# Transposes of the attention sums in halves, and five edits around the last rounds, in a two-layer attention and Fourier kernel

## The chip, the cores and the metric

The kernel runs on one core of a Trainium2 chip. Times are device microseconds of one execution. The kernel before took 1332.05 us (median of 3 runs, 1330.12 to 1336.22). The profile shown below is of one further execution, which took 1332.09 us by itself; the span in its trace, from the first to the last instruction, is 1330.0 us, so 2.1 us lie outside it.

Six names come back all the time. TensorE (PE in the profile) multiplies; PEld is its loading of weights, which overlaps. VectorE (DVE), ScalarE (ACT) and GpSimd (POOL) do the element work. SyncE (SP) only issues DMAs. PSUM is the memory that TensorE writes to: eight banks of 2 KB per partition, so one bank holds 512 fp32 columns of 128 partitions.

## What is computed

Four residual blocks on a sequence of 2048 tokens of width 576, fp32 throughout: attention A, Fourier filter B, A again, B again, each on the layer-normed input.

```python
def _A_ref(x, wqkv, wo):
    H = 32; Dh = D // H; W = 256
    q, k, v = split_heads(x @ wqkv)
    scores = jnp.einsum("bhqd,bhkd->bhqk", q, k) * (Dh ** -0.5)
    mask = (idx[:, None] - idx[None, :] >= 0) & (idx[:, None] - idx[None, :] < W)
    p = _softmax(jnp.where(mask, scores, -1e9), axis=-1)
    return merge_heads(jnp.einsum("bhqk,bhkd->bhqd", p, v)) @ wo

x = x + _A_ref(_layernorm(x), A_wqkv, A_wo)
x = x + _B_ref(_layernorm(x), B_w_r, B_w_i)   # irfft2(rfft2(x) * (w_r + 1j w_i))
x = x + _A_ref(_layernorm(x), A_wqkv, A_wo)
x = x + _B_ref(_layernorm(x), B_w_r, B_w_i)
```

The 32 heads have 18 channels each, and a query sees itself and the 255 tokens before it.

## The kernel before

The program is written out in one fixed order. Each engine takes its own instructions strictly in that order, and an instruction whose inputs or whose buffer are not ready holds up everything behind it on its engine. SyncE's DMA issues are such a queue too.

One attention layer (`layer_a`) has four stages. First the normed input is transposed and split in a high and a low part, and the values are projected (`vps`, L1005). Then q and k are projected in 9 groups of 128 columns (`proj`, accumulators `pj`, L1109). Their weights are loaded by `w_load` and split by `w_split`, in the order of the groups. Then comes the attention itself, and then the output projection (class `Out`, accumulators `ops`, L802), whose first matmuls (`early`) stand directly behind the last matmul of the attention in TensorE's order.

The attention runs over x = 0 to 127: eight groups n of four heads, times sixteen blocks i of 128 tokens. A block needs, for each of its four heads:

- `score_max` (L1160): TensorE writes the block's scores to a bank with tag S, of which there are three, and VectorE takes the row maximum (L1174). It runs ten blocks ahead of the rest.
- `m_rows` (L1182): after four blocks the maxima are transposed (`tpm`), negated by ScalarE and stored by a DMA on SyncE into a row of q, so that the next multiplication already subtracts them.
- `exps` (L1193): TensorE writes scores with the keys on the partitions to a bank with tag E (three of these, too), ScalarE takes the exponent into P, and GpSimd clears what the mask leaves out (L1208, L1211). In the last ten blocks, when most score maxima are done, the second pair of heads uses S banks instead, but not in the last four blocks of all.
- `part` (L1216): TensorE multiplies P with the values, and the sums of exponents come out as a 19th row. The sums of four blocks of queries stand in the four quarters of **one** bank, U (L1434), which is allocated once: blocks 0 and 1 of four in columns 0 to 255, blocks 2 and 3 in columns 256 to 511.

After the fourth block of a chunk c VectorE transposes the whole of U to `us` in squares of 32 by 32 (L1230), so that tokens come to the partitions. `divide` (L1238) takes the reciprocal of the 19th entry on VectorE and multiplies (GpSimd; VectorE for the last n). `back` (L1244) transposes `us` to `o` on VectorE, `store` (L1248) sends `o` to DRAM on SyncE, and after the fourth chunk of a head group `pack` (L1256) copies its 72 used rows within DRAM, with DMAs on GpSimd's queue. The last head group has no pack; its chunks go straight to the tile `o7`.

Two loops order this work. `bursts` (L1330) goes in rounds of three scores and three exponents; up to x of about 104 each round also has a few of the projection's matmuls, and rounds without any follow. `later` (L1311) sets in which following round divide, back, store and pack of a chunk stand: 1, 3, 4 and about 10 rounds on. From x = 118 (`MIX`) a second loop (L1444) goes block by block: exponents of t, then `pv(t-2)`, which is both parts of block t-2, and the waiting steps in between. No score maxima are left there.

`behind` (L1402) puts the preparation of the output projection beside the last 20 blocks: the weights of the output are loaded and split (`out.split`, five times, at t = 110, 112, ... 118; a copy by ScalarE and a subtraction by GpSimd, L752), the constants of the following transform are loaded into buffers that the q and k weights used before (`out.const`, tags wraw, wqh, wql), the packed rows are fetched (`out.attended`, tile `oraw`, last at t = 121 and 122), and at t = 125, 126 and 127 the first three tiles of them are turned and split by VectorE alone (`out.turn`, L787 to L789). The last instructions of the attention are then `pv(126)`, `pv(127)`, the transpose of the last chunk, and its divide and back.

Of the kernel before, what the change touches and what calls it, by code (L numbers as in the profile page):

```python
# [8 lines left out]
F32 = mybir.dt.float32  # L9
F32R = mybir.dt.float32r  # L10
# [5 lines left out]
S, D = 2048, 576  # L16
DF = 289
NF = 290
NT = 16
# [622 lines left out]
NQ = 8  # L642
# [54 lines left out]
def split_w(nc, raw, h, l, eng_l):  # L697
    nc.scalar.copy(h, raw)
    eng_l.tensor_sub(l, raw, h.bitcast(F32))
# [16 lines left out]
class Out:  # L716
# [32 lines left out]
    def split(self, k):  # L749
        c = slice(2 * self.n * k, 2 * self.n * (k + 1))  # L750
        self.nc.scalar.copy(self.w["h"][:, c], self.raw[:, c])
        self.nc.gpsimd.tensor_sub(self.w["l"][:, c], self.raw[:, c], self.w["h"][:, c].bitcast(F32))  # L752

    def const(self, k):

        t = ("wraw", "wraw", "wqh", "wqh", "wql")[k]
        d = self.bp.tile([128, 2, NF], F32R, tag=t, name=f"dc{k}", bufs=2)
        self.nc.sync.dma_start(d.bitcast(F32), self.dc_d[:, 2 * k:2 * k + 2].bitcast(F32))
        self.dcs.append(d)

# [105 lines left out]
def layer_a(tc, ident, eps, bp, big, src, dst, wqk_d, wv_d, wo_d, dc_d, gc_d, dram, copy, wvs, second, spectral, share):  # L866

    nc = tc.nc
    V, A, T, P = nc.vector, nc.scalar, nc.tensor, nc.gpsimd
# [14 lines left out]
    if True:  # L884
# [7 lines left out]
        wt, wraws = {}, {}  # L892

        def w_load(i):
            raw = bp.tile([128, 5, 128], F32, tag="wraw", name=f"wqr{i}", bufs=2)
            nc.sync.dma_start(raw.rearrange("p a b -> p (a b)"), wqk_d[i])
            wraws[i] = raw

        def w_split(i):
            raw = wraws[i]  # L900
            h = bp.tile([128, 5, 128], F32R, tag="wqh", name=f"wqh{i}", bufs=2)
            l = bp.tile([128, 5, 128], F32R, tag="wql", name=f"wql{i}", bufs=2)
            wt[i] = (h, l)
            split_w(nc, raw, h, l, V if i == 2 else P)
            if i + 2 < 9:
                w_load(i + 2)


        with tc.tile_pool(name="a1", bufs=2) as wp, ExitStack() as banks:
            pps = []  # L910
            if not second:
                wraw = wp.tile([128, 5, D], F32, name="wvraw", bufs=1)
# [163 lines left out]
        with ExitStack() as c2:  # L1076
            wp = c2.enter_context(tc.tile_pool(name="a2", bufs=2))
            pp = Banks(tc, c2, "a2p", ("S", "pj"))
# [16 lines left out]
            def proj(i, c, bank=0):  # L1095
# [5 lines left out]
                def mm(s, k):  # L1101
                    wk, p, xk = k
                    if s == 7 and c == 2 and 0 < i < 8:
                        w_split(i + 1)
# [31 lines left out]
            def stack_load(n, c, some=range(4)):  # L1136

                q, k = qs[n % 2], ks_[n % 2]
                cs = slice(c * 512, c * 512 + 512)
                for which, t, parts in ((0, q, (0, 0, 1)), (1, k, (0, 1, 0))):  # L1140
                    for hp in range(2):
                        if 2 * which + hp not in some:
                            continue
                        r0 = 144 * n + 72 * which + 36 * hp
                        for slot, part in enumerate(parts):
                            b = 64 * hp + 18 * slot
                            (P if which and (n == 0 and c > 1 or n == 1 and c == 0) else nc.sync).dma_start(
                                t[b:b + 18, :, cs].bitcast(F32), qk_d[part, r0:r0 + 36, cs].rearrange("(f d) t -> d f t", f=2).bitcast(F32))
# [44 lines left out]
            def exps(x, pair, hp):  # L1193

                n, j = divmod(x, NT)
                q, k = qs[n % 2], ks_[n % 2]
                nq = min(3, NT - j) * 128
                hl_ = 2 * hp + pair
                if hp == pair == 0:
                    pt[n, j] = wp.tile([128, 4, 384], F32, tag="P", name=f"P{n}_{j}", bufs=6)  # L1200
                p = pt[n, j]

                ps = pp.tile([128, 512], F32, name=f"E{x}_{hl_}", **(dict(tag="S", bufs=3) if pair and NX - LEAD <= x < NX - 4 else dict(tag="E", bufs=3)))
                b = 64 * hp
                T.matmul(ps[:, 0:nq], k[b:b + 64, pair, j * 128:j * 128 + 128], q[b:b + 64, pair, j * 128:j * 128 + nq], start=True, stop=True)  # L1205
                A.activation(p[:, hl_, 0:nq], ps[:, 0:nq], AF.Exp, scale=SC)  # L1206
                if hp == pair == 1:
                    P.affine_select(out=p[:, :, 0:128], in_=p[:, :, 0:128], pattern=[[0, 4], [1, 128]], compare_op=ALU.is_ge,  # L1208
                                    fill=0.0, base=0, channel_multiplier=-1)
                    if nq == 384:  # L1210
                        P.affine_select(out=p[:, :, 256:384], in_=p[:, :, 256:384], pattern=[[0, 4], [-1, 128]], compare_op=ALU.is_gt,  # L1211
                                        fill=0.0, base=0, channel_multiplier=1)

            us = {}

            def part(x, half):  # L1216
                n, i = divmod(x, NT)

                e = i - i % 2
                j = (i - 1, i - 2 + 2 * (i % 2))[half]  # L1220
                q0 = e if j < i else i
                q1 = e + 2 if i - 1 == j else q0 + 1
                for h in range(4):
                    if j >= 0:
                        T.matmul(U[32 * h:32 * h + 19, (q0 % 4) * 128:(q0 % 4) * 128 + 128 * (q1 - q0)], vts[n][:, j, h],  # L1225
                                 pt[n, j][:, h, (q0 - j) * 128:(q1 - j) * 128],
                                 start=j == max(e - 1, 0), stop=j == i or (i == e and j == i - 2), skip_group_check=True)
                if half and i % 4 == 3:
                    us[n, i // 4] = u = wp.tile([128, NT, 32], F32, tag="us", name=f"us{n}_{i}", bufs=1)
                    V.transpose(u, U.rearrange("r (p n) -> r n p", n=NT))  # L1230

            def pv(x):
                part(x, 0)
                part(x, 1)

            os = {}

            def divide(n, c):  # L1238
                u = us[n, c]
                rc = wp.tile([128, NT, 1], F32, tag="rc", name=f"rc{n}_{c}", bufs=2)  # L1240
                V.reciprocal(rc, u[:, :, 18:19])
                (V if n == NQ - 1 else P).tensor_mul(u[:, :, 0:18], u[:, :, 0:18], rc.to_broadcast([128, NT, 18]))

            def back(n, c):  # L1244
                os[n, c] = o = wp.tile([128, NT, 32], F32, tag="o", name=f"o{n}_{c}", bufs=2)
                V.transpose(o, us[n, c])

            def store(n, c, engines=None):  # L1248
                o = os[n, c].rearrange("r n p -> r (n p)")
                if n < NQ - 1:  # L1250
                    nc.sync.dma_start(op_d[n, :, c], o)
                    return
                for h in range(4):
                    (engines[h] if engines else nc.sync).dma_start(out.o7[18 * h:18 * h + 18, 512 * c:512 * c + 512], o[32 * h:32 * h + 18])

            def pack(n, h):  # L1256
                a, b = [f.rearrange("e c x -> (e c x)").rearrange("(a b) -> a b", a=16) for f in (o_d[72 * n + 18 * h:72 * n + 18 * h + 18], op_d[n, 32 * h:32 * h + 18])]
                P.dma_start(a, b)

            for k, (i, c) in enumerate(((0, 0), (1, 0), (0, 1), (1, 1), (0, 2), (0, 3), (1, 2), (1, 3))):  # L1260
                for f in proj(i, c, k % 2):
# [8 lines left out]
            NX = NQ * NT  # L1270
            LEAD = 10
# [37 lines left out]
            steps = {}  # L1309

            def later(k, n, c):  # L1311
                for lag, f in zip(later.lags, (divide, back, store)):
                    steps.setdefault(k + lag, []).append((f, n, c))
                if c == 3:
                    for h in range(4):
                        steps.setdefault(k + (10 + 2 * h if n < NQ - 2 else 9 + h // 2), []).append((pack, n, h))

            later.lags = 1, 3, 4

            def lasting(p):  # L1320
                x, half = p
# [8 lines left out]
            def bursts():  # L1330
# [8 lines left out]
                for k in range(-(-len(es) // 3)):  # L1339
# [6 lines left out]
                    for f in e:  # L1346
                        exps(*f)
# [46 lines left out]
                for p in parts:  # L1394
                    part(*p)
                    if p[1] and p[0] % 4 == 3:
                        later(k, *divmod(p[0] // 4, 4))
# [36 lines left out]
            U = pp.tile([128, 512], F32, tag="U", name="U", bufs=1)  # L1434
# [2 lines left out]
                f()  # L1437
                done += 1
            now = -(-4 * MIX // 3)
            later.lags = 1, 3, 4  # L1440
            ahead = [(max(now, 2 * k - now), f) for k in sorted(steps) for f in steps.pop(k)]
            for k, f in ahead:
                steps.setdefault(k, []).append(f)
# [20 lines left out]

            out.early(0, [bank(k, f"ops0_{k}") for k in ("pj", "S")], slice(0, 4))
            divide(NQ - 1, 3)
            back(NQ - 1, 3)
            store(NQ - 1, 3, (nc.sync, nc.scalar, P, nc.sync))
            out.early(0, None, slice(4, 11))
            out.early(1, [bank("S", f"ops1_{k}") for k in range(2)])  # L1470
# [55 lines left out]
```

## Time and profile before

| | us |
|---|---|
| median of 3 runs | 1332.05 |
| the profiled execution | 1332.09 |
| its span | 1330.0 |
| TensorE busy | 1295.2 |
| VectorE busy | 947.2 |
| first and last transpose of U, first layer (start) | 144.1 and 458.3 |
| last transpose of U, second layer (start) | 1139.6 |
| all waits of U's matmuls for VectorE's transposes (8) | 3.3 |
| all waits of exponent scores for ScalarE (8) | 3.7 |

The granted clock of TensorE is 0.996 on average, so the clock explains nothing here. Two kinds of row are read in the following: rows of the timeline, which give a start, a length, engine, line, operation and tiles, and in square brackets the idle time of the engine before it with what ended that; and rows of windows, which give each engine's busy time in a stretch. The timeline merges neighbours of one kind (x2, x3), and the ends of matmuls in it are modelled. A matmul that waits for a bank while the one before is still counted shows as a longer row and not as idle time.

### The profile page before, as it was taken

How to read it: one execution, taken by the hardware profiler on the slowest of the kernel's cores; microseconds unless marked ns; L12 is line 12 of the kernel's file. 1: busy time of each engine (PE TensorE's matmuls, PEld its weight loads, DVE VectorE, ACT ScalarE, POOL GpSimd, SP SyncE). 2: the span in 40 equal slices, each digit the busy share in tenths (PEclk: the TensorE clock that was granted, in tenths of full speed). 3: DMA queues.
4: the chain of work that ended last, by engine and by line, in shares of the span. 5: the costliest groups of instructions: out<-in, count | busy, mean ns of one | idle time of the engine just before them, and what ended most of it. 6: DMA issues, size and time to landing. Idle time of an engine off the chain costs nothing.

```text
span 1330.0 us, 33103 instructions
## 1 busy us (share of the span) xinstructions
PE 1295.2 (97%) x10911; PEld 957.5 (72%) x10911; DVE 947.2 (71%) x3132; ACT 753.5 (57%) x1896; POOL 721.8 (54%) x1212
## 2 busy tenths in 40 slices
PE   9999999999999899999999999999999999999998
PEld 8986666566665599975999975666656654897587
DVE  5417888888889677766674148988888887675755
ACT  5622776677767645533355415677766678573233
POOL 2258666676667643566221295567667668213721
PEclk9999999999999999999999999999999999999999
DMA  6856766665657747688873468566656659497884
GB/s 205 215 161 204 220 206 190 214 201 186 188 162 241 222 120 227 191 282 254 265 251 76 102 208 225 184 213 178 192 175 192 189 173 296 140 346 254 283 260 155
DMA packets 179487, 274.22 MB, mean 206 GB/s; under 512 B 67743, under 2 KB 77727, under 8 KB 177989
## 3 DMA queue, kind: packets, MB, share of 16 engines
q1 hardware_dynamic: 166751, 242.45, 58.4%
q0 software_dynamic: 4912, 14.62, 4.3%
q10 hardware_dynamic: 7654, 15.03, 3.2%
q8 instruction: 88, 1.44, 0.5%
q14 instruction: 82, 0.67, 0.2%
HBM read 164.54 MB, written 114.81 MB: 210 GB/s over the span
## 4 chain that ended last, share of the span: by engine, by line
PE 82%; DMA 4%; POOL 4%; DVE 3%; issue 3%; ACT 2%; SPq 1%; DVEq 0%; ACTq 0%; POOLq 0%
PE pj L1109 18%; PE S L1172 13%; PE U L1225 11%; PE vps L1005 9%; PE ops L802 7%; PE E L1205 5%; PE po L274 4%; PE pq L524 3%; PE p L503 2%; PE pi L600 2%; PE pf L274 2%; PE pz L312 1%; POOL ks L1266 1%; POOL qs L1267 1%; DMA yd<-ye 1%
## 5 line engine op out<-in xcount | busy, mean ns | idle before, releaser
L1174 DVE CUSTOM_DVE_ANT_0 jk<-S,mask 128x384 bf16<-128x384 f32 (+2 forms) x1024 | 488.2, 525 | 72.3 <-PE S L1172 35.9
L1206 ACT ACTIVATE P<-E 128x384 f32<-128x384 f32 (+2 forms) x1024 | 408.2, 476 | 171.9 <-PE E L1205 134.4
L1172 PE MATMUL S<-ks,qs 63*128 63x384 f32 (+2 forms) x1024 | 280.1, 374 | 1.3 <-POOL qs L1267 0.3
L1208 POOL TENSOR_SCALAR_AFFINE_SELECT P<-P 128x512 f32<-128x512 f32 x256 | 163.2, 638 | 190.6 <-ACT P L1206 173.8
L1205 PE MATMUL E<-qs,ks 64*128 64x384 f32 (+2 forms) x1024 | 224.7, 372 | 6.4 <-ACT P L1206 3.7
L1172 PEld LDWEIGHTS S<-ks,qs 63*128 63x128 f32 x1024 | 145.6, 184 | 115.2 <-DVE m L1174 87.2
L1225 PE MATMUL U<-P,vq 128*19 128x128 f32 (+1 forms) x3840 | 188.6, 328 | 5.1 <-DVE us L1230 3.3
L1109 PE MATMUL pj<-xh,wqh 128*128 128x512 f32 x360 | 155.4, 432 | 0.4 <-DVE sg L1127 0.2
L1225 PEld LDWEIGHTS U<-P,vq 128*19 128x19 f32 x3840 | 95.6, 98 | 82.6 <-issue 16.0
L1211 POOL TENSOR_SCALAR_AFFINE_SELECT P<-P 128x512 f32<-128x512 f32 x224 | 142.8, 637 | 0.0
L1205 PEld LDWEIGHTS E<-qs,ks 64*128 64x128 f32 x1024 | 115.6, 185 | 22.5 <-ACT P L1206 16.5
L1109 PE MATMUL pj<-xh,wql 128*128 128x512 f32 x360 | 122.1, 416 | 0.0
L1109 PE MATMUL pj<-xl,wqh 128*128 128x512 f32 x288 | 119.6, 415 | 0.0
L802 PE MATMUL ops<-oroom 128*128 128x290 f32 (+1 forms) x812 | 114.0, 297 | 1.7 <-DVE ofree L848 1.2
L802 PEld LDWEIGHTS ops<-oroom 128*128 128x128 f32 x812 | 110.4, 189 | 2.3 <-ACT ofree L836 1.4
L1109 PEld LDWEIGHTS pj<-xh,wqh 128*128 128x128 f32 x360 | 67.7, 188 | 31.2 <-issue 14.0
L1174 DVE DVE_READ_ACCUMULATOR2_ANT m<- 128x1 f32 x1024 | 85.1, 83 | 0.0
L1121 ACT CAST sg<-pj 128x512 fp32r<-128x512 f32 x72 | 42.4, 589 | 72.9 <-PE pj L1109 66.8
L1109 PEld LDWEIGHTS pj<-xh,wql 128*128 128x128 f32 x360 | 64.2, 188 | 21.9 <-issue 10.8
L1230 DVE STREAM_TRANSPOSE us<-U 128x512 f32<-128x512 f32 x64 | 45.8, 716 | 35.8 <-PE U L1225 35.8
L1109 PEld LDWEIGHTS pj<-xl,wqh 128*128 128x128 f32 x288 | 54.2, 188 | 16.8 <-issue 9.1
L789 POOL TENSOR_TENSOR oroom<-oraw,oroom 64x128 fp32r<-64x128 f32 x26 | 13.9, 536 | 95.8 <-issue 46.1
(509 smaller groups left out, 2290.9 us busy)
## 6 DMA issues: line engine op xcount, KB each, us to landing
qk_d<-sg SPq DMA_DIRECT2D x56, 512.0 KB
qs<-qk_d SPq DMA_DIRECT2D x384, 72.0 KB
ks<-qk_d SPq DMA_DIRECT2D x348, 72.0 KB
op_d<-o SPq DMA_DIRECT2D x56, 256.0 KB
v_d<-vt SPq DMA_DIRECT2D x32, 304.0 KB
vq<-v_d SPq DMA_DIRECT2D x16, 608.0 KB
wt<-in_w SPq DMA_DIRECT2D x16, 580.0 KB
ofree<-x SPq DMA_DIRECT2D x16, 580.0 KB
```

The costliest lines, as they stand in the source:

```text
L274: T.matmul(ps[:, c, 0:NF], tail[r] if si == 4 else hl_(si), dcs[b // 2][r, b % 2], start=mi == si == 0, stop=si == 4)
L802: self.nc.tensor.matmul(self.ps[u][n][:, 0:self.n], x, self.w[p][:, (2 * wk + n) * self.n:(2 * wk + n + 1) * self.n], start=first and i == ...
L1005: T.matmul(ps[:, n, 0:288], xT(xk, c), w[:, wk, n * 288:(n + 1) * 288], start=i == 0, stop=i == len(ks) - 1)
L1109: T.matmul(box["ps"].rearrange("r (n p) -> r n p", n=NT) if second else box["ps"], w[:, wk], x, start=s == 0, stop=s == len(ks) - 1)
L1172: T.matmul(ps[:, 0:N], q[b:b + 63, pair, i * 128:i * 128 + 128], k[b:b + 63, pair, lo:hi], start=True, stop=True)
L1174: V.tensor_tensor_reduce(out=jk[:, 0:N], in0=ps[:, 0:N], in1=mask[:, 384 - N:384], scale=1.0, scalar=-3e38, op0=ALU.add, op1=ALU.max, accu ...
L1205: T.matmul(ps[:, 0:nq], k[b:b + 64, pair, j * 128:j * 128 + 128], q[b:b + 64, pair, j * 128:j * 128 + nq], start=True, stop=True)
L1206: A.activation(p[:, hl_, 0:nq], ps[:, 0:nq], AF.Exp, scale=SC)
L1208: P.affine_select(out=p[:, :, 0:128], in_=p[:, :, 0:128], pattern=[[0, 4], [1, 128]], compare_op=ALU.is_ge, fill=0.0, base=0, channel_mult ...
L1211: P.affine_select(out=p[:, :, 256:384], in_=p[:, :, 256:384], pattern=[[0, 4], [-1, 128]], compare_op=ALU.is_gt, fill=0.0, base=0, channel ...
L1225: T.matmul(U[32 * h:32 * h + 19, (q0 % 4) * 128:(q0 % 4) * 128 + 128 * (q1 - q0)], vts[n][:, j, h], pt[n, j][:, h, (q0 - j) * 128:(q1 - j) ...
L1230: V.transpose(u, U.rearrange("r (p n) -> r n p", n=NT))
```

## The change

Six things are changed; all of them are in both layers.

1. `part` transposes U after every second block, 256 columns at a time, into one half of `us` (which gets two buffers). `back` does the same: its second half stands one round after the first. Order of columns within the halves is such that `o` is the same as before. U stays one bank.
2. `out.split` subtracts with VectorE for k = 3 and 4 (t = 116 and 118) and with GpSimd for k = 0 to 2 as before.
3. `pack` of the last but one head group (n = 6) is issued by SyncE; all others stay with GpSimd.
4. The second pair's exponents use S banks through the last block.
5. q and k weights: the first two raw tiles get buffers of their own, all others share one buffer, so that a load is issued one split later. This makes room for the second `us`.
6. The transform's constants are spread differently over the freed buffers.

```diff
     def split(self, k):
         c = slice(2 * self.n * k, 2 * self.n * (k + 1))
         self.nc.scalar.copy(self.w["h"][:, c], self.raw[:, c])
-        self.nc.gpsimd.tensor_sub(self.w["l"][:, c], self.raw[:, c], self.w["h"][:, c].bitcast(F32))
+        (self.nc.vector if k > 2 else self.nc.gpsimd).tensor_sub(self.w["l"][:, c], self.raw[:, c], self.w["h"][:, c].bitcast(F32))
...
-        t = ("wraw", "wraw", "wqh", "wqh", "wql")[k]
-        d = self.bp.tile([128, 2, NF], F32R, tag=t, name=f"dc{k}", bufs=2)
+        t = ("wraw", "wqh", "wqh", "wql", "wql")[k]
+        d = self.bp.tile([128, 2, NF], F32R, tag=t, name=f"dc{k}", bufs=2 if k else 1)
...
         def w_load(i):
-            raw = bp.tile([128, 5, 128], F32, tag="wraw", name=f"wqr{i}", bufs=2)
+            raw = wp.tile([128, 5, 128], F32, name=f"wqr{i}", bufs=1) if i < 2 else bp.tile([128, 5, 128], F32, tag="wraw", name=f"wqr{i}", bufs=1)
...
-            if i + 2 < 9:
-                w_load(i + 2)
+            if 0 < i < 8:
+                w_load(i + 1)
...
-                ps = pp.tile([128, 512], F32, name=f"E{x}_{hl_}", **(dict(tag="S", bufs=3) if pair and NX - LEAD <= x < NX - 4 else dict(tag="E", bufs=3)))
+                ps = pp.tile([128, 512], F32, name=f"E{x}_{hl_}", **(dict(tag="S", bufs=3) if pair and NX - LEAD <= x else dict(tag="E", bufs=3)))
...
-                if half and i % 4 == 3:
-                    us[n, i // 4] = u = wp.tile([128, NT, 32], F32, tag="us", name=f"us{n}_{i}", bufs=1)
-                    V.transpose(u, U.rearrange("r (p n) -> r n p", n=NT))
+                if half and i % 2:
+                    c, g = divmod(i // 2, 2)
+                    if g == 0:
+                        us[n, c] = wp.tile([128, NT, 32], F32, tag="us", name=f"us{n}_{c}", bufs=2)
+                    V.transpose(us[n, c][:, 8 * g:8 * g + 8], U[:, 256 * g:256 * g + 256].rearrange("r (p a b) -> r a b p", a=8, b=2))
...
-            def back(n, c):
-                os[n, c] = o = wp.tile([128, NT, 32], F32, tag="o", name=f"o{n}_{c}", bufs=2)
-                V.transpose(o, us[n, c])
+            def back(n, c, g):
+                if g == 0:
+                    os[n, c] = wp.tile([128, NT, 32], F32, tag="o", name=f"o{n}_{c}", bufs=2)
+                V.transpose(os[n, c][:, :, 16 * g:16 * g + 16].rearrange("r (a b) p -> r a b p", b=2), us[n, c][:, 8 * g:8 * g + 8])
...
-                P.dma_start(a, b)
+                (nc.sync if n == NQ - 2 else P).dma_start(a, b)
...
-                for lag, f in zip(later.lags, (divide, back, store)):
-                    steps.setdefault(k + lag, []).append((f, n, c))
+                for lag, f, *g in ((1, divide), (3, back, 0), (4, back, 1), (4, store)):
+                    steps.setdefault(k + lag, []).append((f, n, c, *g))
...
             divide(NQ - 1, 3)
-            back(NQ - 1, 3)
+            for g in range(2):
+                back(NQ - 1, 3, g)
             store(NQ - 1, 3, (nc.sync, nc.scalar, P, nc.sync))
```

2 lines of the change are left out of this document (removed).

## The prediction

> **What bounds the kernel now.** I read the page's busy times first, then windows of 10 to 100 us in the attention, then the timeline of TensorE and VectorE there, then both ends of the attention.
>
> ```profile
> PE 1295.2 (97%) x10911; PEld 957.5 (72%) x10911; DVE 947.2 (71%) x3132; ACT 753.5 (57%) x1896; POOL 721.8 (54%) x1212
> ```
>
> TensorE has only 34.8 us of idle time in the span. All that this change can give must come from there, or from stalls that are counted as busy. Windows (stretch, its length, then busy us with instructions for PE, PEld, DVE, ACT, POOL; clock, DMA share, GB/s) show two regimes:
>
> ```profile
> 300.00:400.00 100.00, 99.77 (x992) 61.05 (x988) 85.97 (x331) 70.41 (x178) 65.30 (x98) 1.00 0.57 177
> ```
> ```profile
> 405.00:415.00 10.00, 9.71 (x122) 5.69 (x123) 9.96 (x40) 7.52 (x19) 8.07 (x14) 1.00 0.64 204
> ```
>
> In the long middle of the attention, where rounds carry projection matmuls, TensorE is full and VectorE has slack. From 405 us, when these matmuls are used up, VectorE is full (9.96 of 10) and TensorE runs at its pace.
>
> Hidden stalls stand in the middle. TensorE's rows of two score matmuls, undisturbed and behind a transpose, and VectorE at that place:
>
> ```profile
> 1006.33 0.34 PE L1172 MATMUL S<-ks,qs 63*128 63x384 f32 x2
> ...
> 1069.39 0.67 PE L1172 MATMUL S<-ks,qs 63*128 63x384 f32 x2
> ```
> ```profile
> 1067.44 0.72 DVE L1230 STREAM_TRANSPOSE us<-U 128x512 f32<-128x512 f32 x1 [0.35 <-PE U L1225]
> 1068.08 0.52 DVE L1174 CUSTOM_DVE_ANT_0 jk<-S,mask 128x384 bf16<-128x384 f32 x1
> ```
>
> The transpose holds VectorE for 0.64 us, the three S banks come free that much later, and the pair of scores takes 0.33 us longer. In the two middles (140 to 395 and 820 to 1085 us) I counted the rows of this kind that are longer than 0.44 us and follow a transpose of `us` or `o` within 3 us, 47 of them, from the first to the last:
>
> ```profile
> 151.72 0.48 PE L1172 MATMUL S<-ks,qs 63*128 63x384 f32 x2
> ...
> 1073.16 0.61 PE L1172 MATMUL S<-ks,qs 63*128 63x384 f32 x2
> ```
>
> What they exceed 0.39 us by sums to 10.5 us.
>
> **The change, part by part.** *Price of a half.* It is not in the trace. The whole and its nearest rows by size:
>
> ```profile
> L1230 DVE STREAM_TRANSPOSE us<-U 128x512 f32<-128x512 f32 x64 | 45.8, 716 | 35.8 <-PE U L1225 35.8
> ```
> ```profile
> L1174 DVE CUSTOM_DVE_ANT_0 jk<-S,mask 128x384 bf16<-128x384 f32 x896 | 448.6, 550 | 50.6 <-PE E L1205 31.9 <-PE S L1172 14.9
> ...
> L1174 DVE CUSTOM_DVE_ANT_0 jk<-S,mask 128x128 bf16<-128x128 f32 x64 | 16.6, 285 | 6.2 <-PE S L1172 6.0
> ```
>
> 256 columns cost 550 - 285 = 265 ns in the maxima. A half then holds VectorE for 0.64 - 0.265 = 0.375 us, and a pair of halves 0.11 us longer than a whole. The bounds are 0.32 (exactly half) and 0.64 (no less than a whole); I take 0.375.
>
> *The middle.* Behind each transpose VectorE is late by 0.27 us less. Cutting each of the 47 excesses by at most 0.27 gives 9.2 us. The new half two rounds earlier falls into time in which VectorE would wait for the next score, as the 0.35 us of idle time ahead of 1067.44 shows. Some excesses are exponents that wait for ScalarE, so I take **-7.5 us**, with -3 and -9.2 as bounds.
>
> *The end of the scores* (405 to 437 us, and the same in the second layer). VectorE has no slack, so work is paid in full: about seven transposes in halves, 7 x 0.11 = 0.8 us, and the subtraction of k = 3, for which a similar row (576 columns, fp32r result) gives 0.75:
>
> ```profile
> L949 DVE TENSOR_TENSOR wv<-wvraw,wv 128x576 fp32r<-128x576 f32 x4 | 2.9, 748 | 0.2 <-ACT wv L946 0.2
> ```
>
> Together +1.5 us per layer. The subtraction of k = 4 comes after the last maximum, where VectorE mostly waits; it costs nothing.
>
> *The last blocks.* TensorE's rows in the first layer:
>
> ```profile
> 446.47 0.41 PE L1225 MATMUL U<-P,vq 128*19 128x128 f32 x8 [0.81 <-POOL P L1208]
> 446.81 0.62 PE L1205 MATMUL E<-qs,ks 64*128 64x384 f32 x4
> ...
> 448.14 1.67 PE L1205 MATMUL E<-qs,ks 64*128 64x384 f32 x4
> ```
>
> GpSimd without two packs and two subtractions ends its mask earlier: up to -0.8. Four exponent scores take 1.67 us where banks are short and 0.62 where not, so S banks give up to -1.05 here. Against the +1.5 that leaves -0.35 by the time block 123 is done.
>
> *A new wait at the very end.* U is one bank. Whether TensorE may write one half while VectorE reads the other is seen in how this program treats other banks. ScalarE, VectorE, then ScalarE and VectorE again:
>
> ```profile
> 487.01 0.74 ACT L291 ACTIVATE yh<-pf,ofree 128x578 fp32r<-128x578 f32 x1 [2.11 <-PE pf L274]
> 487.65 0.64 ACT L293 COPY xf<-pf 128x580 f32<-128x580 f32 x1
> ```
> ```profile
> 488.32 0.82 DVE L294 SCALAR_TENSOR_TENSOR yl<-pf,ofree,yh 128x578 fp32r<-128x578 f32 x1 [0.73 <-ACT xf L293]
> ```
> ```profile
> 1280.73 0.40 ACT L617 COPY bs<-po 128x290 f32<-128x290 f32 x1 [1.27 <-issue]
> 1281.03 0.18 ACT L618 ACTIVATE xo<-po 128x2 f32<-128x2 f32 x1
> ```
> ```profile
> 1281.24 0.46 DVE L619 TENSOR_TENSOR xo<-po,bs 128x287 f32<-128x287 f32 x1 [1.33 <-ACT xo L618]
> ```
>
> L294 needs `yh`, ready at 487.75, yet starts at 488.32, when L293 has ended, which merely reads the same bank. L619 starts behind L618, which reads two other columns of its bank. So accesses of two engines are ordered by bank, not by address, and I take the same for a write by TensorE beside a read by VectorE. The Trainium skill, "PSUM — Partial Sum Buffer", section "PSUM bank collisions raise a hardware error", says so outright: disjoint columns of one bank collide, hardware does not arbitrate, so software must order them. The L619 rows agree for two readers; no run here shows a write. By that rule the sum ends at 1330, without it at the first rival's time.
>
> Earlier halves are covered by the exponent scores that stand between two blocks' parts, and VectorE is free there. But the half of blocks 124 and 125 must end before `pv(126)`. On VectorE it stands behind turns 0 and 1 and ahead of turn 2; behind `pv(126)` and `pv(127)` on TensorE stands the whole output projection. VectorE and TensorE, first layer:
>
> ```profile
> 452.20 0.72 DVE L787 CAST oroom<-oraw 128x512 fp32r<-128x512 f32 x1
> ...
> 454.64 0.71 DVE L1246 STREAM_TRANSPOSE o<-us 128x512 f32<-128x512 f32 x1
> ...
> 456.91 0.43 DVE L787 CAST oroom<-oraw 128x512 fp32r<-128x512 f32 x1
> ...
> 458.28 0.72 DVE L1230 STREAM_TRANSPOSE us<-U 128x512 f32<-128x512 f32 x1
> ```
> ```profile
> 456.55 0.40 PE L802 MATMUL ops_pj<-oroom 128*128 128x288 f32 x1
> ```
> ```profile
> L1225 PE MATMUL U<-P,vq 128*19 128x128 f32 (+1 forms) x3840 | 188.6, 328 | 5.1 <-DVE us L1230 3.3
> ```
>
> Turns 0 and 1 end at 456.9. With -0.35 from above and a transpose of blocks 122 and 123 that is a half (-0.27), plus 0.1 for two backs, this becomes 456.4. The half takes 0.4; the 32 matmuls of two blocks take 32 x 188.6 / 3840 = 1.6. TensorE then begins the projection at 458.4 instead of 456.55: **+1.9 us**, with +0.9 if the turns start 1 us earlier, +3.5 if they come later. In the second layer they start when their data land:
>
> ```profile
> 1134.80 0.56 DVE L787 CAST oroom<-oraw 128x512 fp32r<-128x512 f32 x1 [2.03 <-DMA oraw<-o_d]
> ...
> 1138.26 0.43 DVE L787 CAST oroom<-oraw 128x512 fp32r<-128x512 f32 x1
> ```
> ```profile
> 1137.16 0.40 PE L802 MATMUL ops_pj<-oroom 128*128 128x290 f32 x1
> ```
>
> 1138.26 + 0.4 + 1.6 = 1140.3 instead of 1137.16: +3.1. Whatever ScalarE, GpSimd and S banks save there is lost in this wait. I add 0.4 for landings that follow the later end of the scores: **+3.5 us**, with +1.5 and +6 as bounds.
>
> *Pack by SyncE.* Its four issues pass ahead of the store of chunk (7, 0), one load and `attended(3, ...)` on SyncE, and the first waits for the store of `o`, which now stands a round later. Before, SyncE waited about there already:
>
> ```profile
> SPq L1254 <- DMA op_d<-o: 1.4, 1, 1.4
> ```
>
> I take nothing either way beyond the 0.4 above; the second rival prices it.
>
> *The rest.* One raw weight buffer less means that a load starts one group later, still a whole group (56 matmuls) ahead of its split; the old code's load waited for the same split on SyncE. The constants go to buffers whose readers ended with the projection. Both nothing; a late load would hold ScalarE's copy, once per group. The later back and store delay SyncE's next issue by at most a round.
>
> Sum: -7.5 + 1.9 + 3.5 = -2.1 us. The profiled execution took 1332.09 us, 0.04 from the median, so **1330 us**.
>
> **The rivals.**
>
> *First: halves of U are ordered by address.* For it: the two halves share no byte, and no row shows TensorE and VectorE at odds over a bank's other columns. Against: L294 and L619. Then the end gives instead of taking: -1 in the first layer, and -0.3 (only the last chain's shorter half) in the second, where data land at the same time: -8.8 with some of the middle left, 1324 us.
>
> *Second: packing by SyncE brings the turns' data late*, and it ends slower. The store that the pack needs comes a round (about 2 us: three maxima at 0.5 and part of a transpose) later, SyncE stands still until it has landed, and behind it stand the loads that turn 0 needs. Because of the new wait each us passes to TensorE one to one. It decides once the pack leaves SyncE later than GpSimd issued it; 2 us in the first layer and 2 + 1.4 in the second make +5.4, so 1335.5 us. Against: GpSimd itself issued only between its masks, and SyncE had idle time there.
>
> *Third: the stalls do not go.* If a half holds VectorE as long as a whole (0.64), the middle gives nothing and the ends of the scores pay 7 x 0.265 = 1.9 us more each, of which I count half as the other two waits hide some: 1332.1 + 5.4 + 1.9, so 1339.5 us. Against: the maxima fall nearly in proportion to size. This includes that the change does not do what it says.
>
> **How the numbers follow.** Forecast 0.57 (its own range: -9.2 + 0.9 + 1.5 to -3 + 3.5 + 6, so 1325 to 1338.5), first rival 0.20, second 0.14, third 0.09. The range 1322 to 1339 leaves out half of the third and the tails of the others, not over 2 in 10. Faster by over 0.5% (below 1325.4; about what a measurement of this kernel can tell from no change): most of the first rival, 0.17, and a seventh of the forecast, 0.08: 0.25. Slower by over 0.5% (above 1338.8): two thirds of the third, 0.06, a quarter of the second, 0.04, a twentieth of the forecast, 0.03: 0.13. Within: 0.62.
>
> **What would show it.** Right: 128 transposes of each kind with a mean near 450 ns; rows of two scores above 0.44 us behind transposes in the middle go from 47 to a dozen; TensorE idle for 2 to 4 us ahead of its matmuls of blocks 126 and 127 in each layer, put down to `us`, L1230. If that idle time is missing, the first rival holds. If turn 0 starts later than 1134.8 with a wait for `oraw`, the second. If halves last over 600 ns, the third. I would be wrong altogether if VectorE's extra waits for U held up the score banks in the middle.

## The result: slower by 1.5%

The changed kernel takes 1352.47 us (median, 1350.08 to 1353.5) where the kernel before takes 1331.32 us beside it: a ratio of 1.015, 95% interval [1.013, 1.0169]. The forecast was 1330, with 1322 to 1339 as its range, so 21 us came in that the sum did not hold. The profiled execution of the changed kernel took 1351.9 us, with a span of 1350.1; its span stands 20.1 us behind that of the kernel before, and that is what is divided up here.

### The profile after

The busy times and the groups of instructions of the changed kernel, in the form that was shown of the one before:

```profile
PE 1302.0 (96%) x10911; PEld 960.8 (71%) x10911; DVE 959.6 (71%) x3264; ACT 751.6 (56%) x1896; POOL 714.0 (53%) x1200
...
L1225 PE MATMUL U<-P,vq 128*19 128x128 f32 (+1 forms) x3840 | 194.5, 335 | 21.3 <-DVE us L1232 18.3
...
L1232 DVE STREAM_TRANSPOSE us<-U 128x256 f32<-128x256 f32 x128 | 57.3, 448 | 45.3 <-PE U L1225 45.3
```

```profile
L1249 DVE STREAM_TRANSPOSE o<-us 128x256 f32<-128x256 f32 x128 | 54.4, 428 | 0.2
```

TensorE has the same 10911 instructions. Its idle time went from 34.8 to 48.1 us and its busy time rose by 6.8. One row names the idle time: the products into U now wait 18.3 us for the transpose `us` (L1232), against 3.3 before. The 6.8 us of busy time are no work either; they are looked up below, under the last blocks.

Where the 20 us came in is best seen with a clock that both kernels share. VectorE takes 1024 score maxima (`jk`) in the same order in both, so the start of the n-th maximum can be set against the start of the n-th. Of the first layer, the 449th and the 512th, in the timeline of VectorE, first before and then after (the start stands first):

```profile
399.69 0.25 DVE L1174 CUSTOM_DVE_ANT_0 jk<-S,mask 128x128 bf16<-128x128 f32 x1
...
436.33 0.52 DVE L1174 CUSTOM_DVE_ANT_0 jk<-S,mask 128x384 bf16<-128x384 f32 x1
```
```profile
399.71 0.25 DVE L1174 CUSTOM_DVE_ANT_0 jk<-S,mask 128x128 bf16<-128x128 f32 x1
...
442.13 0.51 DVE L1174 CUSTOM_DVE_ANT_0 jk<-S,mask 128x384 bf16<-128x384 f32 x1
```

399.71 - 399.69: after 400 us nothing is gained and nothing lost. 442.13 - 436.33: 5.8 us are lost in the next 37. Done for both layers, with the start of the output projection (`ops_pj`) as the last mark, and set against what the sum had for it:

| stretch | before, us | after, us | difference | predicted |
|---|---|---|---|---|
| middle, layer 1 (1st to 449th maximum) | 295.48 | 295.58 | +0.1 | -3.75 |
| end of the scores, layer 1 (to the 512th) | 36.64 | 42.42 | +5.8 | +1.5 |
| last blocks, layer 1 (to `ops_pj`) | 20.22 | 24.24 | +4.0 | +0.4 |
| middle, layer 2 | 295.98 | 296.50 | +0.5 | -3.75 |
| end of the scores, layer 2 | 36.56 | 43.42 | +6.9 | +1.5 |
| last blocks, layer 2 | 20.46 | 23.84 | +3.4 | +2.0 |

What lies between the rows makes -0.6 us together. Such a stretch is that of one profiled execution: the first middle, taken in kernels that are the same there, differs by some 3 us (294.5 in e8 to 297.3 in e3, two of the experiments below), so the end rows are outside of that and the middle rows are not. Three things are to be explained: a gain of 7.5 us in the middles that isn't there, 9.7 us more than foreseen in the ends of the scores, and 5.0 us more in the last blocks.

**The end of the scores.** VectorE's rows in the changed kernel, then TensorE's:

```profile
415.78 0.55 DVE L1174 CUSTOM_DVE_ANT_0 jk<-S,mask 128x384 bf16<-128x384 f32 x1
416.26 0.45 DVE L1232 STREAM_TRANSPOSE us<-U 128x256 f32<-128x256 f32 x1
416.63 0.40 DVE L1249 STREAM_TRANSPOSE o<-us 128x256 f32<-128x256 f32 x1
418.10 0.56 DVE L1174 CUSTOM_DVE_ANT_0 jk<-S,mask 128x384 bf16<-128x384 f32 x1 [1.07 <-PE E L1205]
```
```profile
415.33 0.41 PE L1225 MATMUL U<-P,vq 128*19 128x128 f32 x8
416.85 0.85 PE L1225 MATMUL U<-P,vq 128*19 128x256 f32 x16 [1.10 <-DVE us L1232]
417.63 0.44 PE L1172 MATMUL S<-ks,qs 63*128 63x384 f32 x1
```

And the same 24 matmuls in the kernel before:

```profile
413.78 1.06 PE L1225 MATMUL U<-P,vq 128*19 128x128 f32 x24
```

Before, TensorE goes from a block's last 8 products straight on to the next block's 16. After, a half transpose lies between them. It is due when the 8 have ended (about 415.7), but VectorE is still at two maxima and reaches it at 416.26; TensorE stands for 1.10 us, and the next score (417.63) comes that much later. By then VectorE has nothing left to do, and stands for 1.07 us in its turn. Two engines in a ring, each full, and each waits for the other once per chunk (in each layer once for 1.44 us, which the trace puts down to GpSimd's mask `P`, and then four times for 0.8 to 1.2 us, put down to `us`). VectorE's idle time between the 449th and the 512th maximum rose from 1.5 to 6.0 us in the first layer and from 1.6 to 6.4 in the second; these 9.3 us are the part of the 12.7 that was not foreseen, to within 0.4.

**The last blocks.** VectorE, then TensorE, first layer:

```profile
459.61 0.87 DVE L788 TENSOR_TENSOR oroom<-oraw,oroom 128x384 fp32r<-128x384 f32 x1
...
463.16 0.41 DVE L1232 STREAM_TRANSPOSE us<-U 128x256 f32<-128x256 f32 x1
```
```profile
463.71 2.72 PE L1225 MATMUL U<-P,vq 128*19 128x256 f32 x32 [4.08 <-DVE us L1232]
466.37 0.40 PE L802 MATMUL ops_pj<-oroom 128*128 128x288 f32 x1
```

That is the wait that was predicted: the half of blocks 124 and 125 stands behind turns 0 and 1. But the 32 products behind it take 2.72 us, not 1.6. The windows of 1 us say why (the column behind POOL's is the clock):

```profile
462.00:463.00 1.00, 0.00 (x0) 0.00 (x0) 0.97 (x3) 0.00 (x0) 0.00 (x0) 0.92 0.74 147
463.00:464.00 1.00, 0.29 (x4) 0.19 (x8) 0.96 (x4) 0.00 (x0) 0.00 (x0) 0.50 0.03 8
464.00:465.00 1.00, 1.00 (x20) 0.67 (x16) 0.76 (x2) 0.00 (x0) 0.00 (x0) 0.50 0.15 37
```

After the idle time the granted clock is 0.50. That is where busy time without work comes from: TensorE's busy time multiplied by the share of the clock that was withheld, added up over the span, is 10.5 us in the changed kernel and 3.4 before. Of the 10.5, 3.7 follow the waits ahead of block 126; the rest is spread over other dips, and how much of it the whole time pays is not shown.

**The middle.** VectorE and TensorE of the changed kernel:

```profile
849.86 0.45 DVE L1232 STREAM_TRANSPOSE us<-U 128x256 f32<-128x256 f32 x1 [0.29 <-PE U L1225]
850.24 0.40 DVE L1249 STREAM_TRANSPOSE o<-us 128x256 f32<-128x256 f32 x1
...
851.97 0.44 DVE L1249 STREAM_TRANSPOSE o<-us 128x256 f32<-128x256 f32 x1
```
```profile
851.63 0.92 PE L1172 MATMUL S<-ks,qs 63*128 63x384 f32 x2
```

The halves do not stand alone: the first half of a transpose back falls into the round of the next half of U, and the two hold VectorE for 0.77 us, longer than a whole one (0.72 by the same count). I grouped the long rows of two scores (excess over 0.39 us, both middles) by the hold ahead of them:

| hold on VectorE | before: holds, excess behind them | changed kernel |
|---|---|---|
| whole transposes, 0.72 us | 98, excess 10.5 us | none |
| one half, 0.44 us | none | 129, excess 4.8 us |
| half of U and half back, 0.77 us | none | 32, excess 9.3 us |

A single half costs 0.04 us where a whole one costs 0.11: better than in proportion, as hoped. But each of the 32 double holds costs 0.29, and the excess rises to 14.0 us. The middles did not become longer by this 3.5 us (+0.6 in the table), so the count shows where TensorE is held up, and not what a stretch costs in the end.

### The profile page after: what moved, and what is told of

It is laid out like the page before. It is cut to its first block, busy times and chain, and to the rows that moved or that the text cites. A ratio compares the mean times of both kernels' runs of the same rounds, so it can differ in the third digit from the quotient of the medians.

```text
span 1350.1 us, 33236 instructions
## 1 busy us (share of the span) xinstructions
PE 1302.0 (96%) x10911; PEld 960.8 (71%) x10911; DVE 959.6 (71%) x3264; ACT 751.6 (56%) x1896; POOL 714.0 (53%) x1200
## 3 DMA queue, kind: packets, MB, share of 16 engines
q8 instruction: 88, 1.44, 0.5%
## 4 chain that ended last, share of the span: by engine, by line
PE 83%; DMA 6%; DVE 4%; ACT 2%; issue 2%; SPq 1%; POOL 1%; DVEq 0%; ACTq 0%; POOLq 0%
PE pj L1109 20%; PE S L1172 13%; PE U L1225 11%; PE vps L1005 9%; PE ops L802 6%; PE E L1205 5%; PE po L274 4%; PE pq L524 3%; PE p L503 2%; PE pf L274 2%; PE pi L600 2%; PE pz L312 1%; ACT P L1206 1%; DMA ofree<-yd 1%; DMA yd<-ye 1%
## 5 line engine op out<-in xcount | busy, mean ns | idle before, releaser
L1225 PE MATMUL U<-P,vq 128*19 128x128 f32 (+1 forms) x3840 | 194.5, 335 | 21.3 <-DVE us L1232 18.3
L1232 DVE STREAM_TRANSPOSE us<-U 128x256 f32<-128x256 f32 x128 | 57.3, 448 | 45.3 <-PE U L1225 45.3
```

Source lines behind the costliest of these rows:

```text
L1232: V.transpose(us[n, c][:, 8 * g:8 * g + 8], U[:, 256 * g:256 * g + 256].rearrange("r (p a b) -> r a b p", a=8, b=2))
```

## Experiments

Theory A: the new waits for the half of U make the loss, in the ends of the scores through VectorE's full queue and in the last blocks through the turns. Rival B: another part of the change does (splits by VectorE, packing by SyncE, score banks). "Stretches" are those of the table above, against the kernel before. All ratios are to the kernel before on the same chip, with a 95% interval.

**e1, e2, e3, e4: which part, and which place.** e1 adds a stop between blocks, in the ends of the scores only (the limit of 433 for 430 keeps the rounds abreast):

```diff
-if took and half == 0 and (x % 4 == 0 or x % NT == 1):
+if took and half == 0 and (x % 2 == 0 or x % NT == 1):
     break
...
-while parts and (took < 430 or source(parts[0]) < e[0][0] - 3 if spread else took == 0 or parts[0][0] % 2 or parts[0][1]):
+while parts and (took < 433 or source(parts[0]) < e[0][0] - 3 if spread else took == 0 or parts[0][0] % 2 or parts[0][1]):
```

> Changed kernel, but in the end of the scores a round stops before the first part of any even block, so that TensorE never goes from a block whose half of U has just been finished straight to the next block in the same round. Theory A (TensorE waits for the new half of U, which stands on VectorE behind the maxima, and VectorE then starves for scores): the 9.3 us of VectorE idle time that came in between the 448th and 511th maximum of each layer (1.5 to 6.0 and 1.6 to 6.4 us) go, 1343 us (1341 to 1346); TensorE's wait of U for us falls from 18.3 to about 10 us. Rival B (weight splits by VectorE, packing by SyncE or the score banks made the loss): within 2 us of the changed kernel, 1352.

e2 and e3 put whole transposes (and whole ones back) in the place of halves, from block 100 on, and everywhere (there the first condition is `True`):

```diff
-if half and i % 2:
+if x >= 100:
+    if half and i % 4 == 3:
+        us[n, i // 4] = u = wp.tile([128, NT, 32], F32, tag="us", name=f"us{n}_{i}", bufs=2)
+        V.transpose(u, U.rearrange("r (p n) -> r n p", n=NT))
+elif half and i % 2:
```

> Changed kernel, but with whole transposes of U and back from block 100 on, halves only before. Theory A: the ends of the scores and the last blocks lose their new waits, 1333 us (1331 to 1337), with the wait of U for us at 3 to 5 us. Rival B: 1345 us or more, since splits, packing and score banks are all still there.

> Changed kernel with whole transposes everywhere; splits, packing, score banks and buffers as changed. Theory A together with 'halves gain nothing in the middle': equal to e2 within 1 us. If the halves did save stalls in the middle as the prediction said (7.5 us), e3 is 7 us above e2. Rival B: 1345 us or more, as e2.

e4 puts the splits back:

```diff
-(self.nc.vector if k > 2 else self.nc.gpsimd).tensor_sub(self.w["l"][:, c], self.raw[:, c], self.w["h"][:, c].bitcast(F32))
+self.nc.gpsimd.tensor_sub(self.w["l"][:, c], self.raw[:, c], self.w["h"][:, c].bitcast(F32))
```

> Changed kernel with all five splits of the output weights on GpSimd again. Theory A: VectorE is rid of 0.75 us in each end of the scores and of 1.2 us ahead of a half in the last blocks, 1349 us (1347 to 1351). Rival B in the form 'the splits are the cause': 1340 us or less.

| run | us | ratio |
|---|---|---|
| e1, stop between blocks | 1343.70 | 1.0089 [1.0064, 1.0115] |
| e2, whole ones from block 100 | 1331.40 | 0.9999 [0.9987, 1.0012] |
| e3, no halves | 1329.94 | 0.9988 [0.9974, 1.0002] |
| e4, splits on GpSimd | 1350.41 | 1.0134 [1.0112, 1.0155] |

e1, e2 and e4 fall where Theory A put them; e3 was to equal e2 within 1 us and is 1.5 us faster, with intervals that overlap. Rival B falls: e2 and e3 keep splits, packing and banks and lose nothing. In e1 the ends of the scores are 1.6 and 1.7 us longer than before, which is the extra work on VectorE alone (+1.5 predicted), and its idle time there is back at 1.8 and 1.7 us. What is left of e1's loss stands in the last blocks (+6.1 and +4.9), as its row of products says (13.7 us of waits, where about 10 were expected):

```profile
L1225 PE MATMUL U<-P,vq 128*19 128x128 f32 (+1 forms) x3840 | 192.8, 334 | 14.0 <-DVE us L1232 13.7
```

e3 is not slower than e2: halves below block 100 gave nothing. In e2 and e3 the last blocks are 1.4 to 2.3 us shorter per layer than before, so the other parts of the change gain there, somewhat more than the 0.7 to 1.1 us by which the ends of the scores are still longer.

**e5, e8, e9: is it the bank?** In e5 the second two blocks of each four go to a bank of their own from block 104 on; e8 has this and whole transposes below block 104. The products into U and the half transpose take `bank_of(e)` for `U`:

```diff
-tag = "E" if done < 70 else "S" if done < len(pj) else "pj"
+tag = "E" if done < 70 else "S"
...
+def bank_of(e):
+    return U2[0] if U2 and e % 4 == 2 else U
...
+if x == 104 and half == 0:
+    U2.append(pp.tile([128, 512], F32, tag="pj", name="U2", bufs=1))
+    V.memset(U2[0], 0.0)
```

> Changed kernel, but from block 104 on the second two blocks of every four are summed in a PSUM bank of their own (the projection's, free by then), so that TensorE never writes the bank that VectorE is transposing. Halves, their places in VectorE's queue, splits and packing as changed. Theory A1 (the order is by bank, and this alone makes TensorE wait): the new waits for us go (under 5 us in all, from 18.3), 1333 us (1330 to 1337), as e2 with a few tenths for the pairs of halves. Rival C (the wait comes from the queue of VectorE whatever the bank, for instance through the shared tile of the results, or from the later packing): 1345 us or more.

> Whole transposes below block 104, from there on halves in two banks as in e5; splits, packing and score banks as changed. Theory A1: as e5 within 2 us, since halves gain nothing below block 104, and as e2 or 1 us below it, 1331 us (1329 to 1333). If halves do save in the middle, e8 is 5 us or more above e5.

Both missed: e5 1348.67 us, 1.0139 [1.0106, 1.0171], and e8 1344.95 us, 1.0097 [1.0068, 1.0126]. By the time alone Theory A's bank would have fallen. TensorE's waits in e5 (total, count, longest) tell another story:

```profile
PE ops_pj L802 <- DVE us L1241: 7.7, 2, 3.9
PE E L1205 <- DMA qs<-mt: 5.5, 3, 2.7
```

No row is left in which U waits for `us`. The waits had moved with the bank: I had borrowed the bank in which the output projection starts, so the projection waited for the transpose in its turn, and the row maxima's transposes, sent to the score banks for that, came late (`qs<-mt`, 0.6 us in the changed kernel). e9 mends both, and has e1's stop:

```diff
+if x == 120 and half == 0:
+    U2.append(pp.tile([128, 512], F32, tag="pj", name="U2", bufs=1))
-out.early(0, [bank(k, f"ops0_{k}") for k in ("pj", "S")], slice(0, 4))
+out.early(0, [bank(k, f"ops0_{k}") for k in ("E", "S")], slice(0, 4))
```

> As e1 (no stop between blocks in the ends of the scores), and blocks 122, 123, 126 and 127 are summed in the projection's bank, which is free by then, while the output projection starts in a bank of the exponents instead; this mends the two side effects of e5 (the output projection waited 3.9 us per layer for the borrowed bank, and an exponent score 2.0 us for the row maxima that had moved to the score banks). Halves, their places in VectorE's queue, splits and packing as changed. Theory A1 (order by bank): TensorE's wait of U for us goes from 13.7 in e1 to under 3 us, the part from the last maximum to the output projection falls to 18 to 20.5 us per layer from 26.3 and 25.4, 1331 us (1328 to 1335). Rival C (another cause in the last blocks): 1340 us or more, as e1.

1333.18 us, 1.0017 [1.0003, 1.0031]. TensorE's wait for `us` in e9:

```profile
PE U L1233 <- DVE us L1240: 2.2, 4, 0.8
```

13.7 us became 2.2, and the last blocks take 20.7 and 20.5 us where e1 had 26.3 and 25.4. All halves, their places on VectorE, the splits and the packing are those of e1. So TensorE waits because it writes the bank that VectorE reads, though in columns that VectorE does not read; a half in a bank of its own costs hardly any wait. (The last blocks of e9 are still 2.3 to 2.5 us per layer longer than those of e2. The granted clock was 0.50 in e9 from 439.0 to 449.3 and from 1118.3 to 1128.5 us, within these blocks, and in e2 for only 3.4 us, in the second layer. That may be why, but no run tests it.)

**e6, e10, e11: the middle.** e6 is the kernel before with transposes of 32 columns instead of 512 below block 100 (the rest of those results is left out):

```diff
-V.transpose(u, U.rearrange("r (p n) -> r n p", n=NT))
+V.transpose(u[:, 0:1], U[:, 0:32].rearrange("r (p n) -> r n p", n=1))
-V.transpose(o, us[n, c])
+V.transpose(o[:, 0:1], us[n, c][:, 0:1])
```

> Kernel before, but below block 100 each transpose of U and each transpose back takes 32 columns instead of 512 (the rest of the result is left at a constant), so that VectorE holds its queue for some 0.1 us instead of 0.64. Theory D (the score pairs' stalls behind the transposes set the middle's pace, as the prediction had it): the two middles lose most of the 10.5 us that were counted, 1321 to 1324 us. Rival E (TensorE's stalls there are made up for before the next one, so that something else sets the pace of the middle): within 3 us of before, 1328 to 1332.

1322.86 us, 0.9936 [0.9914, 0.9958]: the middles lose 4.6 and 4.3 us, 8.9 together. The transposes' holds do set the middle's pace; rival E falls. That 8.9 lies near the 10.5 that were counted is partly luck: the excess of all long pairs in the middles fell only from 11.8 to 7.0 us, so the pairs show a part of what the holds cost. Then e10, which is e2 with the first half back a round earlier wherever it would meet the next half of U:

```diff
+early = 2 if 16 * n + 4 * c < 100 and k + 3 in {(4 * x + 7) // 3 + 2 for x in range(0, MIX - 2, 2)} else 3
-for lag, f, *g in ((1, divide), (3, back, 0), (4, back, 1), (4, store)):
+for lag, f, *g in ((1, divide), (early, back, 0), (4, back, 1), (4, store)):
```

> As e2 (halves below block 100, whole ones behind), but where the first half of the transpose back would fall into the round of the next half of U, it is issued one round earlier. Theory F (in a third of the cases the two halves stand back to back and hold VectorE for 0.77 us, and these 32 holds make 9.3 of the 14 us of stalled score pairs in the changed kernel, while a single half costs 0.03 to 0.05 us): the double holds vanish, the stalls fall to some 4 us, and the middles give 5 to 7 us: 1326 us (1323 to 1328). Rival G (halves gain nothing however they stand): 1331, as e2.

1324.94 us, 0.9957 [0.9944, 0.9971]: 5.6 us better than e2 by the ratios. Its 194 halves all stand alone, with 9.0 us of excess where e2 had 13.6, and each middle is 2.4 us shorter than before. Over all the runs this is clear of the spread: both middles together take 590.9 to 593.2 us in the four kernels with whole transposes there (before, e3, e7, e8), 590.3 to 592.1 in the seven with the changed kernel's halves, and 586.6 and 585.8 in e10 and e11. So the size of the hold is what counts, and the double holds ate the gain. e11 also puts splits and packing back on GpSimd:

> As e10, with the splits and the packing on GpSimd as in the kernel before, so that of the change only the score banks and the halves below block 100 are left. If splits and packing cancel (they cost 0.7 to 1.1 us in an end of the scores and gave 0.8 to 1.8 us behind it, e3 against e7): within 2 us of e10. With theory F: 1322 us (1320 to 1326); with rival G: 1327.5, as e7.

1324.51 us, 0.9954 [0.9939, 0.9968], as e10 within the intervals; splits and packing cancel. e10 and e11 are faster than both kernels. How much of that the halves give in the whole time is less sure: e7 (below) has the score banks of e11 and no halves, and e11 is only 2.0 us better by the ratios, with intervals that overlap, where its middles are 5.3 us shorter.

**e7: the score banks alone**, in the kernel before:

```diff
-if pair and NX - LEAD <= x < NX - 4
+if pair and NX - LEAD <= x
```

> Kernel before with one part of the change: score banks for the exponents to the end. If the gain of 1.4 to 2.3 us per layer that e2 and e3 show after the last maximum is that of the banks: 1327 us (1325 to 1329). If it is that of the splits on VectorE: 1330 to 1331.

1327.49 us, 0.9969 [0.9952, 0.9986], as expected for the banks; but its last blocks are only 0.6 and 0.5 us shorter than before, and the rest of the 4 us can't be told from what one profile differs from the next.

**e12: what the clock adds.** 16 matmuls that nobody reads stand ahead of the products of block 126, in the time that TensorE would wait:

```diff
+if t - 2 == NX - 2:
+    fill = pp.tile([128, 512], F32, tag="pj", name="fill", bufs=1)
+    for _ in range(16):
+        T.matmul(fill[:, 0:128], ident, ident, start=True, stop=True)
 pv(t - 2)
```

> Changed kernel with 16 matmuls of 128 columns that nobody reads (some 0.14 us each) on TensorE ahead of the products of block 126, where it stood idle for 4.08 and 3.24 us. Theory H (the granted clock of 0.50 that followed this idle time is its consequence, and is a loss of its own: 1.3 us in the first layer, 2.6 us busy at half the clock between 463.7 and 466.3, and 2.4 us in the second, 4.9 us between 1154.2 and 1159.1): the clock stays at 1.00 there, the 32 matmuls of blocks 126 and 127 take 1.6 instead of 2.7 us, and the time falls by 2 to 4 us to 1349 (1348 to 1351). Rival I (the clock dips for another reason, such as the transfers just before): the 32 matmuls still take 2.7 us, and the time is 1352 to 1353.

1348.21 us, 1.0134 [1.0112, 1.0155], with more work than the changed kernel (1.015). TensorE's rows:

```profile
460.37 3.84 PE L1456 MATMUL fill<-ident 128*128 128x128 f32 x32
465.62 1.50 PE L1225 MATMUL U<-P,vq 128*19 128x256 f32 x32 [1.40 <-DVE us L1232]
467.04 0.40 PE L802 MATMUL ops_pj<-oroom 128*128 128x288 f32 x1
```

(Each filler is recorded as two.) The 32 products take 1.50 us in place of 2.72, in the second layer too (2.77 in the changed kernel), and no lowered clock follows in either. So the first half of Theory H holds: the idle time lowers the clock, and the lowered clock makes these products long. What that costs in the whole time is not shown. It is 2 us by the ratios and 4 by the medians, but the intervals of the two ratios overlap, and the last blocks take 24.5 and 23.6 us, hardly other than the 24.2 and 23.8 of the changed kernel. In the first layer the products began 1.9 us later than there, as turn 0 waited 2.81 us for a transfer (1.07 in the changed kernel); that is more than the 1.2 us which the shorter row gives. The dips in the changed kernel at 442 to 446, 1118 to 1122 and 1139 to 1142 us have no filler of their own and were not tried.

## Why the prediction was wrong

- **Price of a half**: right. 448 and 428 ns against "near 450".
- **Order by bank**: right, and e9 shows it for the last blocks. The first rival (by address) falls.
- **The wait at the very end**: right in place (TensorE idle 4.08 and 3.24 us ahead of block 126), too small in size: +7.4 us in the two last blocks where the sum had +2.4. The clock of 0.50 behind the wait (1.1 us more for the 32 products) was not in the sum; nor were the turns that start later, since the ends of the scores ended later.
- **"Earlier halves are covered by the exponent scores that stand between two blocks' parts, and VectorE is free there"**: this is the step that failed first, and with it the slack assumed in the ends of the scores. It is true of the middle, where a round stops ahead of each even block. In the ends of the scores a round goes from one block straight to the next, and the prediction's own window showed VectorE at 9.96 of 10 us there. Its extra work was sized right (+1.5 predicted, +1.6 and +1.7 in e1); the ring of waits between two full engines, 4.4 and 4.8 us, was not seen. The wait that the prediction named for blocks 126 and 127 holds for every half; it was worked out at one place only.
- **The middle, -7.5 us**: wrong, +0.6 measured. The stalls are real (e6) and shorter holds do shorten them (e10), though even with all halves apart the middles gain 4.8 us and not 7.5. The sign that was named in advance, that the 47 long pairs go to a dozen, failed: by the same rule there are 69 in the changed kernel. The step "behind each transpose VectorE is late by 0.27 us less" took every half to stand alone; a third of the halves of U are followed by a half back in the same round, which the lags 3 and 4 and the two or three rounds from one half of U to the next give away in the code. The third rival's outcome (no gain in the middle) came true without its reason.
- **The second rival**: the turns' data were not the cause. In the second layer turn 0 (1149.35 us) had no wait for `oraw`, and e3, with the packing on SyncE, isn't slower than before. In the first layer of the changed kernel turn 0 did wait 1.07 us for a transfer, and in e1 longer, as VectorE's row there shows:

```profile
457.57 0.43 DVE L787 CAST oroom<-oraw 128x512 fp32r<-128x512 f32 x1 [3.46 <-DMA ofree<-o]
```

  The half of blocks 124 and 125 stood behind it, and TensorE waited 5.82 us. So late data count only through that half: a contribution, and not the cause.
- **Score banks and GpSimd's relief**: right in sign; with whole transposes all the other parts together give 1.4 to 2.3 us per layer in the last blocks (e2, e3), where the sum had 1.85.

## What to carry to other kernels

Where a buffer of one bank is emptied in pieces, each piece is a new meeting point of the two engines, so look at every place in the program order where the writer goes on at once, and ask how long the reader's queue is there; where both engines are full, a wait on one comes back as a wait on the other. Cutting a long hold into short ones helps only if the pieces stay apart: list the rounds in which each piece lands before counting the gain. When an experiment misses, read whether its own edit made the new wait before the theory is dropped (e5 against e9).

## What the hardware showed that was not expected

TensorE had stood still for less than 2 us when its granted clock fell. In the second layer it stopped at 1151.0 us and went on at 1154.2, and these are its products and the windows of the changed kernel (clock behind POOL's column):

```profile
1154.22 2.77 PE L1225 MATMUL U<-P,vq 128*19 128x256 f32 x32 [3.24 <-DVE us L1232]
```
```profile
1151.00:1152.00 1.00, 0.00 (x0) 0.00 (x0) 0.99 (x3) 0.97 (x3) 1.00 (x3) 1.00 1.12 272
1152.00:1153.00 1.00, 0.00 (x0) 0.00 (x0) 0.95 (x3) 0.96 (x2) 0.57 (x1) 0.67 0.41 82
1153.00:1154.00 1.00, 0.00 (x0) 0.00 (x0) 0.99 (x4) 0.00 (x0) 0.00 (x0) 0.50 0.03 8
...
1158.00:1159.00 1.00, 1.00 (x6) 1.00 (x5) 0.96 (x3) 0.00 (x0) 0.00 (x0) 0.50 0.00 0
1159.00:1160.00 1.00, 1.00 (x8) 1.00 (x8) 0.11 (x1) 0.00 (x0) 0.57 (x1) 0.92 0.00 0
```

By these rows the clock fell at about 1152.3, 1.4 us into the gap, and came back at about 1159.2, 4.9 us after TensorE had taken up work again. In the first layer it fell 3.2 us into the gap and came back 2.6 us after work began again. It also fell near 442.4 us, where TensorE had stood for 0.80 and 0.79 us within the last 2.3 us. These are its windows there:

```profile
440.00:441.00 1.00, 0.20 (x10) 0.06 (x2) 1.00 (x4) 0.34 (x1) 0.00 (x0) 1.00 1.06 364
441.00:442.00 1.00, 0.56 (x4) 0.24 (x4) 1.00 (x5) 0.55 (x2) 0.00 (x0) 1.00 1.09 365
442.00:443.00 1.00, 0.65 (x8) 0.39 (x12) 0.97 (x5) 0.71 (x2) 0.93 (x2) 0.68 1.09 385
443.00:444.00 1.00, 1.00 (x14) 0.44 (x6) 0.61 (x1) 0.00 (x0) 0.30 (x1) 0.50 1.04 392
```

Whether the short gaps did it there is not shown: e12 tests the long waits alone. The Trainium skill, "TensorE: Matmul & The Clock Gate", section "The HAM clock gate (the "warmup" mystery)", gives half the clock after a window of about 3.4 us idle and the full one after as long busy, with windows that run free of the program. The first layer's fall agrees, and the returns, 2.6 and 4.9 us after work began again, lie to both sides of it. The second layer's fall after 1.4 us, and the one among short gaps, came sooner than that, and there the measurement decides.
